# Seven block products in one more output stage, a later query load, and another order in the last stage

## The chip, the core and the metric

The program runs on one core of a Trainium2 chip. Its engines work side by side and wait for each other through semaphores: TensorE (PE, matrix products into the PSUM banks), VectorE (DVE), ScalarE (ACT), GpSimd (POOL) and SyncE (SP). POOL, SP and ACT also issue DMA transfers. The metric is device time in microseconds, the median of several runs of the program. The profile is one execution, whose span runs from its first to its last instruction.

## What is computed

A linear attention with cosine weights feeds a gated feed-forward block. Only what matters here is shown:

```python
def phi(x, c, s):
    r = np.maximum(x, 0.0)
    return np.concatenate([r * c, r * s], axis=-1)
q_p = phi(q, cos_w, sin_w)
k_p = phi(k, cos_w, sin_w)
kv = np.einsum('bhsf,bhsd->bhfd', k_p, v)
z = np.sum(k_p, axis=2)
num = np.einsum('bhsf,bhfd->bhsd', q_p, kv)
den = np.einsum('bhsf,bhf->bhs', q_p, z)[..., None] + 1e-06
attn_out = num / den
x = attn_out.transpose(0, 2, 1, 3).reshape(B * S, H * D)
g = x @ w_gate
silu = g * (1.0 / (1.0 + np.exp(-g)))
val = x @ w_val
out = silu * val @ w_out
```

The batch is 8, the heads 8, the sequence 576, the head dimension 64; so x has 4608 rows of 512, and d_ff is 1536. All inputs and the output are float32; the kernel multiplies in 16 bits.

## The kernel before

The 4608 rows are worked through in nine groups (`tg` 0 to 8) of 512 tokens, each of four tiles of 128. A group has a feed-forward stage of 12 slices (`fc`), which leaves the hidden activations in `ht`, and an output stage, which multiplies `ht` by `w_out` (`wo_sb`). Between the pieces of both, "slots" hang the attention work that the next groups need: 16 slots in a group, 12 in the feed-forward stage and 4 in the output stage. Groups 0 and 1 have a plain output stage, twelve products with 512 columns for each tile:

```python
def ffn_out(t, f0=0, f1=None, queues=None):
    ...
    r = t % OUT * P
    for fc in range(f0, f1):
        nc.tensor.matmul(out=o_ps[t], lhsT=ht[:, fc, r:r + P], rhs=wo_sb[:, fc],
                         start=(fc == 0), stop=(fc == FC - 1))
    ...
    if t % 2 == 0:
        nc.scalar.mul(out=ob_of(t), in_=ps, mul=DOWN)
    else:
        nc.vector.tensor_single_scalar(out=ob_of(t), in_=ps, scalar=DOWN, op=ALU.mult)
    store(t, queues=queues)
```

Groups 2 to 8 split the product into 2 by 2 blocks and form it from seven block products in place of eight (Strassen's method in Winograd's form). This needs four sums of blocks of the weights (`weight_sum`, T1 to T4, once for the kernel) and four sums of blocks of `ht` in each group (`token_sum`, S1 to S4). `HC` is 6, so one `product` is 12 matmuls of 256 columns:

```python
def sums_behind(fc):
    for n, lo, hi in {7: ((3, 0, 4),), 8: ((1, 0, 4),), 9: ((2, 0, 4),), 10: ((4, 0, 4), (3, 4, 6)),
                      11: ((1, 4, 6), (2, 4, 6))}.get(fc, ()):
        token_sum(n, lo, hi)

def out_by_quarters(tg, slot_of):
    last = tg == NTG - 1
    ...
    def product(to, a, b, first):
        for kc in range(HC):
            for i in range(2):
                nc.tensor.matmul(out=to[i][:, 0] if len(to) == 2 else to[0][:, i],
                                 lhsT=a[:, kc, i * P:(i + 1) * P], rhs=b[:, kc], ...)
    ...
    nb = 2 if last else 1
    a = home("a", fills=True)
    product(a, aq[:, 0, 0], bq[:, 0, 0], True)
    b = home("b", nb, seeded=True)
    for p_, o_ in each(b, a[0]):
        nc.scalar.copy(out=p_, in_=o_)
    e = home("e", fills=True)
    product(e, S3, T3, True)
    nc.scalar.mul(out=C22, in_=e[0], mul=DOWN)
    c = home("c", seeded=True)
    free("e")
    product(b, S2, T2, False)
    ...                                     # VectorE: c from C22 and b
    token_sum(4, 0 if tg in GATE else 4, 6)
    slot_of(0)
    product(a, aq[:, 1, 0], bq[:, 1, 0], False)
    copied("act", C11, a)
    free("a")
    if last:
        store_two(t0, slice(0, HD))
    slot_of(1)
    product(b, S1, T1, False)
    ...                                     # VectorE: C22 from b
    if last:
        store_two(t0 + 2, slice(HD, d_model))
    product(c, aq[:, 1, 1], T4, False)
    copied("act", C21, c)
    free("c")
    if last:
        store_two(t0 + 2, slice(0, HD))
    else:
        for t in (t0 + 2, t0 + 3):
            store(t, queues=queues)
    slot_of(2)
    product(b, S4, bq[:, 1, 1], False)
    copied("dve", C12, b)
    ...
    for t in (t0, t0 + 1):
        store(t, *((slice(HD, d_model), (nc.sync, nc.scalar)) if last else (slice(0, d_model), queues)))
    slot_of(3)
```

In the last group `b` lies in two banks, one for each tile of the pair, and `store_two` issues its two transfers on SP and on ACT. The loop over the groups, and the loads that run ahead:

```python
def load_behind(b):
    nc.gpsimd.tensor_copy(out=hold2, in_=phit[b - 1][0:1, :, 0, 0, 0])   # POOL waits for the turned q
    if b < AHEAD:                     # AHEAD = 5
        load(b, "q")
    if b > 3:
        load_kv(b)
    if AHEAD <= b + 1 < B:
        load(b + 1, "q")

for tg in range(1, NTG):
    s0 = SLOTS * tg
    if tg in GATE:                    # 5 to 8: gate product by seven block products too
        if not loose[0]:
            loose[0] = True
            rows[0] = max(used) + 1
        ffn_by_quarters(tg, lambda i: slot(s0 + i))
    for fc in range(FC) if tg not in GATE else ():
        ffn_fc(tg, fc)
        if tg > 1:
            sums_behind(fc)
        slot(s0 + fc)
    if tg > 1:
        out_by_quarters(tg, lambda i: slot(s0 + FC + i))
        continue
    for i in range(OUT):
        ffn_out(tg * OUT + i, queues=(nc.gpsimd, nc.gpsimd))
        weight_sum(i)
        slot(s0 + FC + i)
```

PSUM has eight banks, and `take` deals them out when the program is written. From group 5 on (`loose`) it gives the free bank whose last use, by an estimate kept in rows of work, lies furthest back:

```python
def take(n, hold=None, fills=False, seeded=False):
    taken = {x for r in held.values() for x in r}
    if loose[0]:
        free = [b for b in range(8) if b not in taken]
        if n == 1:
            bs = [min((b for b in free if filled[b] or not seeded), key=lambda b: used[b])]
        else:
            b0 = min((b for b in free if b + 1 in free), key=lambda b: max(used[b:b + 2]))
            bs = [b0, b0 + 1]
    ...
```

Of the kernel before, what the change touches and what calls it, by code (L numbers as in the profile page):

```python
# [18 lines left out]
def kernel(  # L19
# [10 lines left out]
    nc = tc.nc  # L30
    B, H, S, D = q.shape
    P = 128
# [18 lines left out]
    KH = KC // 2  # L51
    GATE = (5, 6, 7, 8)
    AHEAD = 5
    WSUM = (29, 38, 48, 64)
    ROW = {2: ([16, 16, 17, 17], 18, (20, 21, 21, 22), 8), 3: ([12, 12, 13, 13], 18, (17, 20, 21, 21), 6), 4: ([12, 12, 14, 14], 14, (13, 16, 17, 18), 5), 5: ([12, 12, 12, 14], 14, (14, 16, 17, 17), 5), 6: ([6, 8, 11, 12], 12, (13, 14, 15, 18), 3), 7: ([6, 6, 7, 7, 8, 8, 9, 9, 10, 10, 11, 11, 12, 12, 13, 13, 14, 14], 16, (12, 13, 14, 15), 3)}
    TILES = {2: (2, 9, 10, 11), 3: (5, 8, 10, 11), 4: (5, 7, 9, 11), 5: (3, 4, 7, 9), 6: (0, 2, 5, 7), 7: (0, 1, 5, 7), 8: (0, 3, 5, 7)}
    KVONE = (2, 5)
    LATER = {2: (0, 1, 3, 4, 7, 8), 3: (0, 1, 3, 4, 7, 8), 4: (0, 1, 3, 4, 7, 8), 5: (0, 1, 3, 4, 7, 8), 6: (0, 1, 3, 4, 7, 8), 7: (0, 1, 3, 4, 7, 8), 8: (0, 1, 3, 4, 7, 8)}
    LATE = dict(M=44, V=87, O=131, X=26, x=150, v=(190, 250, 120, 150), e=130, a=90, c=170, b=110, k=120)

# [21 lines left out]

    filled = [False] * 8
    loose = [False]
    rows = [0]

    def take(n, hold=None, fills=False, seeded=False):

        taken = {x for r in held.values() for x in r}
        if loose[0]:  # L90
            free = [b for b in range(8) if b not in taken]
            if n == 1:
                bs = [min((b for b in free if filled[b] or not seeded), key=lambda b: used[b])]
            else:
                b0 = min((b for b in free if b + 1 in free), key=lambda b: max(used[b:b + 2]))
                bs = [b0, b0 + 1]
            if hold is not None:
                held[hold] = bs
            for b in bs:
                filled[b] = fills or seeded  # L100
            touch(bs)
            return banks[:, bs[0]] if n == 1 else banks[:, bs[0]:bs[0] + 2]
        free = [b for b in range(0, 8, n) if not any(b <= x < b + n for x in taken)
                and (filled[b] or not seeded)]

        b0 = min(free, key=lambda b: (n == 1 and hold is not None and hold[0] == "o" and b ^ 1 not in taken,
                                      sorted(used[b:b + n], reverse=True)))
        if hold is not None:
            held[hold] = range(b0, b0 + n)
        filled[b0:b0 + n] = [fills or seeded] * n  # L110
        touch(range(b0, b0 + n))
        return banks[:, b0] if n == 1 else banks[:, b0:b0 + n]
# [649 lines left out]
            (queues or (nc.sync, nc.sync))[e].dma_start(out=out_v[idx // NC, idx % NC][:, cols],  # L762
                                                        in_=ob_of(t)[e * SH:(e + 1) * SH, cols])

    def store_two(t, cols):
        for e in range(2):
            (b, c), (b1, _) = divmod(2 * t + e, NC), divmod(2 * t + 2 + e, NC)
            assert b == b1
            (nc.sync, nc.scalar)[e].dma_start(
                out=out_v[b, c:c + 3:2, :, cols].rearrange("c p f -> p c f"),  # L770
                in_=obs[t // 2][e * SH:(e + 1) * SH, :, cols])

# [40 lines left out]
# [8 lines that stand above are left out]
        queues = (nc.gpsimd, nc.gpsimd) if tg > 0 else None  # L821
        t0 = tg * OUT
        for t in (t0, t0 + 2):
            ob_of(t)
        C11, C12 = (obs[t0 // 2][:, :, x * HD:(x + 1) * HD] for x in range(2))
        C21, C22 = (obs[t0 // 2 + 1][:, :, x * HD:(x + 1) * HD] for x in range(2))

        def home(nm, parts=1, **kw):
            return [take(1, ("o", tg, nm, i), **kw).rearrange("p (t x) -> p t x", x=HD) for i in range(parts)]

        def free(nm, parts=1):
            for i in range(parts):
                give_back(("o", tg, nm, i))

        def product(to, a, b, first):
            rows[0] += LATE["O"]
            for kc in range(HC):
                for i in range(2):
                    nc.tensor.matmul(out=to[i][:, 0] if len(to) == 2 else to[0][:, i],  # L839
                                     lhsT=a[:, kc, i * P:(i + 1) * P], rhs=b[:, kc],  # L840
                                     start=first and kc == 0 and i == 0,
                                     stop=kc == HC - 1, skip_group_check=True)

        def each(ps, *others):
            if len(ps) == 1:
                return [(ps[0], *others)]
            return [(ps[i][:, 0:1], *(o[:, i:i + 1] for o in others)) for i in range(2)]

        def copied(eng, o, ps, x=DOWN):
            for p_, o_ in each(ps, o):  # L850
                if eng == "act":
                    nc.scalar.mul(out=o_, in_=p_, mul=x)  # L852
                else:
                    nc.vector.tensor_single_scalar(out=o_, in_=p_, scalar=x, op=ALU.mult)
# [13 lines that stand above are left out]
        for p_, o_, x_ in each(b, c[0], C22):  # L868
            nc.vector.scalar_tensor_tensor(out=o_, in0=x_, scalar=UP, in1=p_, op0=ALU.mult, op1=ALU.add)
# [9 lines that stand above are left out]
        for p_, x_ in each(b, C22):  # L879
            nc.vector.scalar_tensor_tensor(out=x_, in0=p_, scalar=DOWN, in1=x_, op0=ALU.mult, op1=ALU.add)  # L880
        if last:
            store_two(t0 + 2, slice(HD, d_model))
        product(c, aq[:, 1, 1], T4, False)
        copied("act", C21, c)
        free("c")
        if last:
            store_two(t0 + 2, slice(0, HD))
        else:
            for t in (t0 + 2, t0 + 3):
                store(t, queues=queues)  # L890
        slot_of(2)
        product(b, S4, bq[:, 1, 1], False)
        copied("dve", C12, b)
        free("b", nb)
        for t in (t0, t0 + 1):
            store(t, *((slice(HD, d_model), (nc.sync, nc.scalar)) if last else (slice(0, d_model), queues)))
        slot_of(3)
# [31 lines left out]
    def at(s, *fns):  # L929
        plan.setdefault(s, []).extend(fns)  # L930
# [8 lines left out]
    def turn(t, fast=False):  # L939
        return lambda: x_turn(t, fast)  # L940
# [83 lines left out]
    def load_2():  # L1024

        nc.gpsimd.tensor_copy(out=hold2, in_=xT[1][0:1, 0, 0, 0:2])
        for nm in ("k", "v"):
            load(2, nm)

    at((0, 1), turn(4), load_2)  # L1030
    at((1, 0), turn(5), a_(6, 0))
    at((1, 1), a_(6, 1))
# [16 lines left out]
    def load_behind(b):  # L1049

        nc.gpsimd.tensor_copy(out=hold2, in_=phit[b - 1][0:1, :, 0, 0, 0])
        if b < AHEAD:
            load(b, "q")
        if b > 3:
            load_kv(b)
        if AHEAD <= b + 1 < B:
            load(b + 1, "q")

    def load_kv(b):
# [6 lines left out]
        load_kv(3)  # L1066


    for n in range(4):
        at(WSUM[n], lambda n=n: gate_weight_sum(n))  # L1070
    for tg in GATE:
# [31 lines left out]
    for tg in range(1, NTG):  # L1103
        s0 = SLOTS * tg
        if tg in GATE:
# [3 lines that stand above are left out]
            ffn_by_quarters(tg, lambda i: slot(s0 + i))  # L1109
        for fc in range(FC) if tg not in GATE else ():  # L1110
            ffn_fc(tg, fc)
            if tg > 1:
                sums_behind(fc)
            slot(s0 + fc)
        if tg > 1:
            out_by_quarters(tg, lambda i: slot(s0 + FC + i))
            continue
        for i in range(OUT):
            ffn_out(tg * OUT + i, queues=(nc.gpsimd, nc.gpsimd))
            weight_sum(i)  # L1120
            slot(s0 + FC + i)
    assert not plan, sorted(plan)


# [28 lines left out]
```

## Time and profile before

| What | us |
|---|---|
| device time, median of 3 runs (lowest to highest) | 314.07 (313.59 to 314.17) |
| span of the profiled execution | 312.5 |
| TensorE busy | 303.3 |
| VectorE busy | 235.9 |
| ScalarE busy | 154.7 |
| GpSimd busy | 66.0 |

The granted TensorE clock was 0.999 over the span. Busy time is the time in which at least one instruction of an engine was under way. "L839" in a line of the profile is line 839 of the kernel: L605 is the plain feed-forward product, L663 and L676 the gate and value products of groups 5 to 8, L780 the plain output stage, L839 the seven block products of the output stage, L354 the k-by-v product, L485 the q-by-kv product. A wait is put down to the operation that released it.

### The profile page before, as it was taken

Reading aid. Unit: us, or ns where it says so; the run is one execution under the profiler, and the core shown is the slowest. Engines: PE = TensorE matmul, PEld = TensorE weight load, DVE = VectorE, ACT = ScalarE, POOL = GpSimd, SP = SyncE. Lnnn points to the kernel's source line nnn. Section 1 sums busy time; section 2 is a strip of 40 time slices with the busy share of each in tenths; the row PEclk is TensorE's granted clock in tenths of the full one; section 3 lists DMA queues with packets and bytes.
Section 4 is the critical chain, followed back from the end, with each engine's and each line's share of the span. In section 5 each row is a group of like instructions: output and inputs, shape, how many; then the busy total and the mean of one; then the engine's idle time right before and its main releaser. Section 6 shows DMA issues by size and latency. Waiting matters only on the chain.

```text
span 312.5 us, 6945 instructions
## 1 busy us (share of the span) xinstructions
PE 303.3 (97%) x2768; PEld 196.9 (63%) x2768; DVE 235.9 (75%) x474; ACT 154.7 (49%) x294; POOL 66.0 (21%) x118
## 2 busy tenths in 40 slices
PE   8799999999999999999999999999999999999992
PEld 3587465445445486547654686768767876786682
DVE  7774678787876988587887887898789569855771
ACT  7454556673435446435545454778543344334520
POOL 7754202001420405030413031202200220040000
PEclk9999999999999999999999999999999999999999
DMA  7999999998798898979496979790991141022005
GB/s 257 222 198 196 206 205 128 236 134 111 115 235 125 137 186 142 167 107 202 84 187 90 200 124 197 79 149 19 169 135 33 23 131 36 20 63 71 2 1 134
DMA packets 72976, 41.08 MB, mean 131 GB/s; under 512 B 49904, under 2 KB 69872, under 8 KB 72944
## 3 DMA queue, kind: packets, MB, share of 16 engines
q0 software_dynamic: 24880, 24.91, 46.6%
q1 hardware_dynamic: 47472, 15.21, 30.8%
q10 hardware_dynamic: 592, 0.52, 0.6%
q8 instruction: 21, 0.34, 0.4%
q14 instruction: 11, 0.09, 0.1%
HBM read 37.75 MB, written 9.44 MB: 151 GB/s over the span
## 4 chain that ended last, share of the span: by engine, by line
PE 92%; DMA 3%; DVE 2%; SPq 1%; ACT 1%; issue 0%; DVEq 0%; ACTq 0%
PE banks L605 33%; PE banks L839 21%; PE banks L676 13%; PE banks L663 11%; PE banks L780 6%; PE banks L354 3%; DMA ht<-in_k_dram 3%; PE banks L485 2%; PE banks L535 1%; SPq L171 1%; PE banks L466 1%; DVE ht L681 1%; PE banks L577 0%; DVE x L512 0%; ACT phit L417 0%
## 5 line engine op out<-in xcount | busy, mean ns | idle before, releaser
L611 ACT ACTIVATE sg<-banks 128x512 bf16<-128x512 f32 (+2 forms) x68 | 37.2, 548 | 52.4 <-PE banks L605 49.9
L605 PE MATMUL banks<-xT,wg_sb 128*128 128x512 f16 (+2 forms) x272 | 62.0, 354 | 0.0
L605 PE MATMUL banks<-xT,wv_sb 128*128 128x512 f16 (+2 forms) x272 | 62.0, 354 | 0.0
L616 DVE TENSOR_TENSOR ht<-sg,banks 128x512 f16<-128x512 bf16 (+2 forms) x68 | 41.7, 622 | 21.9 <-PE banks L605 15.4
L762 POOL DMA_DIRECT2D out_dram<-ob x56 | 29.5, 534 | 116.8 <-ACT ob L852 111.2
L676 PE MATMUL banks<-xT,wv_sb 128*128 128x512 f16 x192 | 48.6, 379 | 0.0
L605 PEld LDWEIGHTS <-wv_sb 128*128 128x128 f16 x272 | 26.1, 98 | 26.1
L605 PEld LDWEIGHTS <-wg_sb 128*128 128x128 f16 x272 | 24.8, 98 | 21.5
L839 PEld LDWEIGHTS <-ht 128*128 128x128 f16 x336 | 32.8, 98 | 4.8
L681 DVE TENSOR_TENSOR ht<-sg,banks 128x512 f16<-128x512 bf16 x48 | 31.0, 681 | 3.3 <-ACT sg L669 3.3
L676 PEld LDWEIGHTS <-wv_sb 128*128 128x128 f16 x192 | 18.8, 98 | 13.3
L839 PEld LDWEIGHTS <-sums 128*128 128x128 f16 x252 | 24.7, 98 | 2.9
L669 ACT ACTIVATE sg<-banks 128x512 bf16<-128x512 f32 x36 | 20.5, 590 | 11.8 <-PE banks L663 11.8
L780 PE MATMUL banks<-wo_sb,ht 128*128 128x512 f16 x96 | 22.7, 379 | 0.0
L512 DVE TENSOR_TENSOR x<-banks,rec 128x512 f16<-128x512 f32 (+1 forms) x32 | 21.6, 674 | 1.3 <-PE banks L466 0.3
L663 PEld LDWEIGHTS <-wgs_sb 128*128 128x128 f16 x192 | 17.8, 98 | 7.4 <-issue 0.6
L663 PE MATMUL banks<-kvt,wgs_sb 128*128 128x256 f16 x144 | 21.6, 273 | 0.4 <-DVE x L512 0.4
L839 PE MATMUL banks<-wo_sb,ht 128*128 128x256 f16 x168 | 20.6, 273 | 0.0
L304 DVE TENSOR_TENSOR v<-raw_v,tab 128x1152 bf16<-128x1152 bf16 x27 | 19.8, 753 | 0.3 <-ACT raw_v L902 0.3
L839 PE MATMUL banks<-wt_sb,sums 128*128 128x256 f16 x168 | 19.5, 273 | 0.0
L839 PE MATMUL banks<-wt_sb,ht 128*128 128x256 f16 x168 | 19.5, 273 | 0.0
L852 ACT ACTIVATE ob<-banks 128x512 f32<-128x512 f32 x14 | 8.4, 598 | 22.1 <-PE banks L839 19.0
(125 smaller groups left out, 409.0 us busy)
## 6 DMA issues: line engine op xcount, KB each, us to landing
out_dram<-ob POOLq DMA_DIRECT2D x56, 128.0 KB, 4.1
raw_k<-in_k_dram POOLq DMA_DIRECT2D x7, 576.0 KB, 6.0
raw_q<-in_q_dram POOLq DMA_DIRECT2D x6, 576.0 KB, 11.3
raw_v<-in_v_dram POOLq DMA_DIRECT2D x6, 576.0 KB, 9.3
wo_sb<-in_moe_w_out_dram POOLq DMA_DIRECT2D x3, 512.0 KB, 12.8
out_dram<-ob SPq DMA_DIRECT2D x11, 128.0 KB, 5.8
wg_sb<-in_moe_w_gate_dram POOLq DMA_DIRECT2D x5, 256.0 KB, 9.1
wv_sb<-in_moe_w_val_dram POOLq DMA_DIRECT2D x5, 256.0 KB, 9.6
```

Of the source, the lines that this page charges most:

```text
L304: nc.vector.tensor_tensor(out=v2s[b == 1][:, g, :, :, 0:D], in0=(first if b == 0 and g == 0 else {"v": raw_of(b, "v")})["v"][:, g].unsquee ...
L512: nc.vector.tensor_tensor(out=st["x", t].rearrange("p (y e d) -> p e y d", e=2, d=D)[:, :, ys], in0=ps[:, :, 0:2 * J * D1].rearrange("p e ...
L605: nc.tensor.matmul(out=st["f", tg, fc, lo][i], lhsT=(wg_sb, wv_sb)[i][:, kc, fs], rhs=xT[tg][:, ts, kc], start=(kc == 0), stop=(kc == KC - 1))
L611: nc.scalar.activation(out=sg[:, 0:n], in_=st["f", tg, fc, lo][0], func=AF.Silu, scale=DOWN)
L616: nc.vector.tensor_tensor(out=ht[:, fc, r:r + n], in0=st.pop(("s", tg, fc, lo))[:, 0:n], in1=ps[1], op=ALU.mult)
L663: nc.tensor.matmul(out=to[:, i], lhsT=a[:, c, 2 * u + i], rhs=x[:, :, c], start=first and i == 0 and c == 0, stop=c == KH - 1, skip_group_ ...
L669: nc.scalar.activation(out=gates[u, w][:, :, j * HT:(j + 1) * HT], in_=src, func=AF.Silu, scale=DOWN)
L676: nc.tensor.matmul(out=val[u, i, w], lhsT=wv_sb[:, kc, fc * P:(fc + 1) * P], rhs=xT[tg][:, :, kc], start=(kc == 0), stop=(kc == KC - 1))
L681: nc.vector.tensor_tensor(out=ht[:, fc], in0=gates[u, w][:, i], in1=val.pop((u, i, w)), op=ALU.mult)
L762: (queues or (nc.sync, nc.sync))[e].dma_start(out=out_v[idx // NC, idx % NC][:, cols], in_=ob_of(t)[e * SH:(e + 1) * SH, cols])
L780: nc.tensor.matmul(out=o_ps[t], lhsT=ht[:, fc, r:r + P], rhs=wo_sb[:, fc], start=(fc == 0), stop=(fc == FC - 1))
L839: nc.tensor.matmul(out=to[i][:, 0] if len(to) == 2 else to[0][:, i], lhsT=a[:, kc, i * P:(i + 1) * P], rhs=b[:, kc], start=first and kc == ...
```

## The change

Group 1 takes the output stage of seven block products, which spares one block product in eight. Its four weight sums must then be there before the stage begins, so they move from that stage into slots of group 0's output stage and group 1's feed-forward stage (`TSUM`), and group 1's token sums are added behind its slices 7 to 11. The first query load that runs ahead (batch element 5) no longer follows directly on the loads for element 4; it waits until the last turned x tile that group 3 will read, made during group 2, has landed. Four numbered picks of a PSUM bank (`SECOND`) take the second-best bank in place of the best, batch element 4 takes two single banks for its k-by-v product (`KVONE`), and several slots move by one or two. In the last group the block C21 is scaled on VectorE in place of ScalarE, the two stores of C22 are both issued on SP, and the last product is ordered by halves, so that the first of its two banks is complete before the second is begun.

```diff
-    WSUM = (29, 38, 48, 64)
-    ROW = {... 3: ([12, 12, 13, 13], 18, (17, 20, 21, 21), 6), 4: ([12, 12, 14, 14], 14, (13, 16, 17, 18), 5), 5: ([12, 12, 12, 14], 14, (14, 16, 17, 17), 5), ...}
-    TILES = {2: (2, 9, 10, 11), 3: (5, 8, 10, 11), ...}
-    KVONE = (2, 5)
+    WSUM = (31, 38, 48, 64)
+    ROW = {... 3: ([12, 12, 14, 14], 18, (17, 20, 21, 21), 6), 4: ([12, 12, 12, 14], 14, (15, 16, 17, 18), 5), 5: ([12, 12, 12, 14], 15, (14, 16, 16, 17), 4), ...}
+    TILES = {2: (0, 9, 10, 11), 3: (5, 9, 10, 11), ...}
+    SECOND = (31, 37, 38, 79)
+    TSUM = [(2, 2), (2, 3), 18, 19]
+    KVONE = (2, 4, 5)
 ...
+            picks[0] += 1
+            other = picks[0] in SECOND
 ...                                        # n == 1, and the same for a pair
-                bs = [min((b for b in free if filled[b] or not seeded), key=lambda b: used[b])]
+                bs = sorted((b for b in free if filled[b] or not seeded), key=lambda b: used[b])
+                bs = bs[min(other, len(bs) - 1):][:1]
 ...
-        def product(to, a, b, first):
+        def product(to, a, b, first, halves=False):
-            for kc in range(HC):
-                for i in range(2):
+            steps = [(kc, i) for kc in range(HC) for i in range(2)]
+            for kc, i in sorted(steps, key=lambda x: x[1]) if halves else steps:
 ...
-            store_two(t0 + 2, slice(HD, d_model))
+            store_two(t0 + 2, slice(HD, d_model), (nc.sync, nc.sync))
         product(c, aq[:, 1, 1], T4, False)
-        copied("act", C21, c)
+        copied("dve" if last else "act", C21, c)
 ...
-        product(b, S4, bq[:, 1, 1], False)
+        product(b, S4, bq[:, 1, 1], False, last)
 ...
+    for n in range(4):
+        at(TSUM[n], lambda n=n: weight_sum(n))
 ...                                        # in load_behind
-        if AHEAD <= b + 1 < B:
+        if AHEAD < b + 1 < B:
 ...
+    def load_ahead():
+        nc.gpsimd.tensor_copy(out=hold2, in_=xT[AHEAD - 2][0:1, OUT - 1, 0, 0:2])
+        load(AHEAD, "q")
+
+    at(SLOTS * (AHEAD - 3) + FC, load_ahead)
 ...                                        # in the loop over the groups
-            if tg > 1:
-                sums_behind(fc)
+            sums_behind(fc)
             slot(s0 + fc)
-        if tg > 1:
-            out_by_quarters(tg, lambda i: slot(s0 + FC + i))
-            continue
-        for i in range(OUT):
-            ffn_out(tg * OUT + i, queues=(nc.gpsimd, nc.gpsimd))
-            weight_sum(i)
-            slot(s0 + FC + i)
+        out_by_quarters(tg, lambda i: slot(s0 + FC + i))
```

More of the change, by code (lines that the diff above doesn't have):

```diff
@@ L53 @@
     AHEAD = 5
-    WSUM = (29, 38, 48, 64)
-    ROW = {2: ([16, 16, 17, 17], 18, (20, 21, 21, 22), 8), 3: ([12, 12, 13, 13], 18, (17, 20, 21, 21), 6), 4: ([12, 12, 14, 14], 14, (13, 16, 17, 18), 5), 5: ([12, 12, 12, 14], 14, (14, 16, 17, 17), 5), 6: ([6, 8, 11, 12], 12, (13, 14, 15, 18), 3), 7: ([6, 6, 7, 7, 8, 8, 9, 9, 10, 10, 11, 11, 12, 12, 13, 13, 14, 14], 16, (12, 13, 14, 15), 3)}
-    TILES = {2: (2, 9, 10, 11), 3: (5, 8, 10, 11), 4: (5, 7, 9, 11), 5: (3, 4, 7, 9), 6: (0, 2, 5, 7), 7: (0, 1, 5, 7), 8: (0, 3, 5, 7)}
-    KVONE = (2, 5)
+    WSUM = (31, 38, 48, 64)
+    ROW = {2: ([16, 16, 17, 17], 18, (20, 21, 21, 22), 8), 3: ([12, 12, 14, 14], 18, (17, 20, 21, 21), 6), 4: ([12, 12, 12, 14], 14, (15, 16, 17, 18), 5), 5: ([12, 12, 12, 14], 15, (14, 16, 16, 17), 4), 6: ([6, 8, 11, 12], 12, (13, 14, 15, 18), 3), 7: ([6, 6, 7, 7, 8, 8, 9, 9, 10, 10, 11, 11, 12, 12, 13, 13, 14, 14], 16, (12, 13, 14, 15), 3)}
+    TILES = {2: (0, 9, 10, 11), 3: (5, 9, 10, 11), 4: (5, 7, 9, 11), 5: (3, 4, 7, 9), 6: (0, 2, 5, 7), 7: (0, 1, 5, 7), 8: (0, 3, 5, 7)}
+    SECOND = (31, 37, 38, 79)
+    TSUM = [(2, 2), (2, 3), 18, 19]
+    KVONE = (2, 4, 5)
     LATER = {2: (0, 1, 3, 4, 7, 8), 3: (0, 1, 3, 4, 7, 8), 4: (0, 1, 3, 4, 7, 8), 5: (0, 1, 3, 4, 7, 8), 6: (0, 1, 3, 4, 7, 8), 7: (0, 1, 3, 4, 7, 8), 8: (0, 1, 3, 4, 7, 8)}
@@ L84 @@
     loose = [False]
+    picks = [0]
     rows = [0]
@@ L91, in take @@
             free = [b for b in range(8) if b not in taken]
+            picks[0] += 1
+            other = picks[0] in SECOND
             if n == 1:
-                bs = [min((b for b in free if filled[b] or not seeded), key=lambda b: used[b])]
-            else:
-                b0 = min((b for b in free if b + 1 in free), key=lambda b: max(used[b:b + 2]))
+                bs = sorted((b for b in free if filled[b] or not seeded), key=lambda b: used[b])
+                bs = bs[min(other, len(bs) - 1):][:1]
+            else:
+                b0 = sorted((b for b in free if b + 1 in free), key=lambda b: max(used[b:b + 2]))
+                b0 = b0[min(other, len(b0) - 1)]
                 bs = [b0, b0 + 1]
@@ L763, in store, with store_two @@
                                                         in_=ob_of(t)[e * SH:(e + 1) * SH, cols])
-    def store_two(t, cols):
+    def store_two(t, cols, queues=None):
         for e in range(2):
@@ L768, in store_two @@
             assert b == b1
-            (nc.sync, nc.scalar)[e].dma_start(
+            (queues or (nc.sync, nc.scalar))[e].dma_start(
                 out=out_v[b, c:c + 3:2, :, cols].rearrange("c p f -> p c f"),
@@ L833, in free @@
                 give_back(("o", tg, nm, i))
-        def product(to, a, b, first):
+        def product(to, a, b, first, halves=False):
             rows[0] += LATE["O"]
-            for kc in range(HC):
-                for i in range(2):
[L839 to L842, printed above, removed]
+            steps = [(kc, i) for kc in range(HC) for i in range(2)]
+            for kc, i in sorted(steps, key=lambda x: x[1]) if halves else steps:
+                nc.tensor.matmul(out=to[i][:, 0] if len(to) == 2 else to[0][:, i],
+                                 lhsT=a[:, kc, i * P:(i + 1) * P], rhs=b[:, kc],
+                                 start=first and kc == 0 and i == 0,
+                                 stop=kc == HC - 1, skip_group_check=True)
         def each(ps, *others):
```

## The prediction, made before the result was known

> **What bounds the kernel now.** I read the shares of busy time first, then the chain of work in order of time, then TensorE's own waits, and last the timeline of the stages that the change touches.
>
> ```profile
> PE 303.3 (97%) x2768; PEld 196.9 (63%) x2768; DVE 235.9 (75%) x474; ACT 154.7 (49%) x294; POOL 66.0 (21%) x118
> ...
> L780 PE MATMUL banks<-wo_sb,ht 128*128 128x512 f16 x96 | 22.7, 379 | 0.0
> ...
> L839 PE MATMUL banks<-wt_sb,sums 128*128 128x256 f16 x168 | 19.5, 273 | 0.0
> ```
>
> TensorE is the bound: it is busy for 97% of the span, and the chain gives it 92%. The second and third line are the two kinds of output stage. Their means, 379 and 273 ns, are no costs, since neighbours overlap; what a stage costs has to be read as elapsed time, from the chain:
>
> ```profile
> 77.72 10.36 PE banks L780 x48
> ...
> 111.34 9.20 PE banks L839 x84
> ```
>
> The columns are start, length and number of instructions. The first is group 1's plain stage, 48 matmuls in 10.36 us, 216 ns each. The second is group 2's stage of seven block products, 84 in 9.20 us, 109.5 ns each; the later ones read 9.19, 9.17, 9.17, 9.17 and 9.17 us. TensorE's waits are few:
>
> ```profile
> PE banks L441 <- DVE wgs_sb L433: 1.1, 1, 1.1
> PE banks L208 <- DVE zeros L203: 1.0, 1, 1.0
> PE banks L466 <- DVE wt_sb L454: 0.6, 1, 0.6
> PE banks L663 <- DVE x L512: 0.4, 1, 0.4
> PE banks L354 <- DVE ht L681: 0.3, 1, 0.3
> ```
>
> The first three lie in the opening, which the change leaves alone. The last two lie at 191.8 and 193.7 us, in group 5, where TensorE waits for banks that VectorE has not yet read: 0.75 us in all. What is left is the end:
>
> ```profile
> 302.79 2.78 PE L839 MATMUL banks<-wt_sb,ht 128*128 128x256 f16 x24
> 302.99 0.60 ACT L852 ACTIVATE ob<-banks 128x512 f32<-128x512 f32 x1 [2.02 <-PE banks L839]
> 303.61 4.35 SPq L769 DMA_DIRECT2D out_dram<-ob  x3
> 303.62 3.08 ACTq L769 DMA_DIRECT2D out_dram<-ob  x2
> 304.19 0.76 DVE L880 SCALAR_TENSOR_TENSOR ob<-banks,ob 128x256 f32<-128x256 f32 x2 [0.72 <-PE banks L839]
> ...
> 305.41 1.47 PE L839 MATMUL banks<-wo_sb,sums 128*128 128x256 f16 x12
> 306.74 0.60 ACT L852 ACTIVATE ob<-banks 128x512 f32<-128x512 f32 x1 [3.15 <-issue]
> 306.81 0.76 DVE L854 TENSOR_SCALAR ob<-banks 128x256 f32<-128x256 f32 x2 [1.87 <-PE banks L839]
> 307.37 0.64 ACTq L769 DMA_DIRECT2D out_dram<-ob  x1
> 308.06 1.20 SPq L762 DMA_DIRECT2D out_dram<-ob  x2
> 308.10 1.45 ACTq L762 DMA_DIRECT2D out_dram<-ob  x2
> ```
>
> TensorE ends at 306.88, the span at 312.5: a tail of 5.6 us. The product for C21 is done at about 305.5, yet ScalarE scales it at 306.74, because its queue was busy with stores from 303.62 to 306.70. So C21's stores are issued at 307.37, the four stores of C12 queue behind them, and the last begins at 309.00 (the ACT pair is 0.80 and 0.55 us). VectorE had C12 ready at 307.57.
>
> [...] Here one issue is 0.55 to 0.66 us on either queue (one took 2.36), and four in a row are much of the tail.
>
> **Part 1, group 1's output stage.** It trades 48 matmuls of 10.36 us for 84 of 9.19 us: **−1.17 us**, straight on the path, if TensorE isn't held. Its sums are on VectorE, so I walked VectorE's queue through the end of group 1, whose times before are (slices 7 and 8, the casts of the k-by-v product, slices 9 and 11):
>
> ```profile
> 70.04 1.28 DVE L616 TENSOR_TENSOR ht<-sg,banks 128x512 f16<-128x512 bf16 x2
> 71.74 1.23 DVE L380 CAST kv<-banks 64x130 bf16<-64x130 f32 x4 [0.42 <-PE banks L354]
> 73.60 0.69 DVE L616 TENSOR_TENSOR ht<-sg,banks 128x512 f16<-128x512 bf16 x1 [0.64 <-PE banks L605]
> ...
> 77.57 0.69 DVE L616 TENSOR_TENSOR ht<-sg,banks 128x512 f16<-128x512 bf16 x1 [0.26 <-PE banks L605]
> ```
>
> Start to start, a slice's product takes 0.61 us, a sum of 1024 elements 0.61, one of 512 about 0.38 (so in group 2), and an x tile 1.04. Slice 7 then ends at 70.65, its sum at 71.26, slice 8 at 71.87, the next sum at 72.48, the casts at 73.7, slice 9 at 74.3, its sum at 74.9, an x tile at 75.95, slice 10 at 76.55, two sums at 77.55, an x tile at 78.6, slice 11 at 79.2, the last two sums at about 79.95. The first product needs only even slices, the second S3, which is there at 77.55. The third needs S2, at 77.72 + 2 × 1.31 = 80.34. So VectorE is 0.4 us early, and in group 2, at the same point, it is as early (113.4 for 113.96). The weight sums, 4 × 0.95 us, fall where VectorE has room: an idle 1.24 us before 54.54, then slices 0 to 4 with idle stretches of 0.6 to 1.1 us. I add nothing for them.
>
> **Part 2, the last stage.** With C21 on VectorE, which is free from 304.95, it is ready at 305.5 + 0.69 = 306.2, its stores go out at about 306.25 instead of 307.37 and end at 306.9. Both stores of C22 lie on SP, at 304.97 and 305.6, done by 306.2, so that ACT isn't held by them. The first half of the last product is complete at 305.41 + 6 × 0.109 = 306.06, its copy of 0.42 us ends at 306.6; the second copy, at TensorE's end, ends at 307.25. The C12 stores then start at 306.95 and 307.55 on each queue, and the last at 307.6 instead of 309.00: 1.4 us. The transfers get denser: about 1 MB must leave after 305, and the DMA engines moved at most 276 GB/s in any microsecond there, so I keep **−1.2 us**. TensorE's work in this stage stays 84 matmuls.
>
> **Part 3, the held load, the slots and the bank picks.** The load for element 5 was issued at 104.72, right behind three loads of 576 KB, and is used by ScalarE only in group 3's output stage, at 143 us. Held until group 3's last x tile has landed, at about 117, it has some 25 us for 7 to 11 us of transfer. It relieves the transposes of x in group 2, but no TensorE wait stands there: 0. Of the 0.75 us of waits in group 5, none of the four altered picks falls on the bank concerned (counting calls, that is about the 12th to 14th in group 5; the altered are 31, 37, 38 and 79). But the order of use with which group 5 starts is new, as are its slots in group 4. I give it four chances in ten, so **−0.3 us**.
>
> The sum is −1.17 − 1.2 − 0.3 = −2.67, and 314.07 − 2.67 = 311.40. The time outside the span, 1.6 us, stays.
>
> **Rivals.** (A) VectorE becomes the bound at the end of group 1: my margin is only 0.4 us on a walk with some ten steps. If a matmul waits for S2 or for a bank, 0.3 to 1 us is lost of part 1, and the time is 311.7 to 312.4. The 75% busy VectorE and 86% in the stretch from 71.7 to 79.2 speak for it, group 2, which is as full and has no wait, against. (B) The tail is set by transfers, not issues: if landing rather than issue sets the end, denser stores land 0.5 to 1 us later than I assume, and the time is 311.9 to 312.4. For it speaks that the DMA engines are at 0.97 from 309 to 310; against, that they are at 0.37 in the microsecond before. (C) The new bank order makes new waits in groups 5 to 8, or the shifted schedule lets a q or x transpose land late; four hand-chosen picks show how sensitive this is. Each wait seen is 0.3 to 0.4 us; three would make it 312.5. (D) The group 5 waits vanish whole, as the slots were retuned as a set: 310.95.
>
> **Range and chances.** The two large parts are mechanical, and the rivals cost more than (D) adds. I take 311.4, with 310.4 to 312.9 eight times in ten. Two per cent, 6.3 us, is more than all parts together, and a loss of that size would need a wait in every group: faster 0.01, within 2% 0.985, slower 0.005.
>
> **What would show it.** Right: a chain without L780 in group 1 but an L839 piece of 84 near 9.2 us there, no wait of TensorE for `sums`, `wt_sb` or `ob`; C21's scaling on VectorE before 306.3 on the old clock of time, less part 1; the last store issued within 0.8 us of TensorE's end (2.1 before); a tail of 4.2 to 4.5 us instead of 5.6. Wrong: a group 1 stage over 9.6 us, more or longer waits of TensorE than two beyond the opening, or a tail over 5 us although the issues are early.

## The result and the profile after

The changed kernel takes 311.62 us (311.47 to 311.79) against 314.06 us before: a ratio of 0.9924, 95% interval 0.9912 to 0.9937. The forecast was 311.4. The span of the profiled execution fell from 312.5 to 309.8 us.

The lines of the changed kernel that answer to those shown of before are these: from the page the busy shares, from the chain in order of time group 1's and group 2's output stages (start, length, number of matmuls; L846 is now the seven block products), and TensorE's waits (total, times, longest).

```profile
PE 302.2 (98%) x2804; PEld 200.5 (65%) x2804; DVE 240.9 (78%) x486; ACT 155.5 (50%) x297; POOL 67.7 (22%) x119
```

```profile
77.58 9.17 PE banks L846 x84
...
110.01 9.19 PE banks L846 x84
```

```profile
PE banks L215 <- DVE zeros L210: 1.0, 1, 1.0
PE banks L448 <- DVE wgs_sb L440: 0.7, 1, 0.7
PE banks L473 <- DVE wt_sb L461: 0.6, 1, 0.6
PE banks L670 <- DVE x L519: 0.4, 1, 0.4
```

Group 1's stage starts almost where it did (77.58 for 77.72) and takes 9.17 us in place of 10.36. Of the two waits in group 5 the one of 0.33 us is gone, the one of 0.42 us is still there. The timeline of the last stage:

```profile
301.84 3.31 SPq L776 DMA_DIRECT2D out_dram<-ob  x4
301.84 3.36 ACTq L776 DMA_DIRECT2D out_dram<-ob  x2
302.42 0.76 DVE L887 SCALAR_TENSOR_TENSOR ob<-banks,ob 128x256 f32<-128x256 f32 x2 [0.73 <-PE banks L846]
303.63 1.47 PE L846 MATMUL banks<-wo_sb,sums 128*128 128x256 f16 x12
303.83 1.08 DVE L861 TENSOR_SCALAR ob<-banks 128x512 f32<-128x512 f32 x2 [0.66 <-PE banks L846]
305.14 0.42 DVE L861 TENSOR_SCALAR ob<-banks 128x256 f32<-128x256 f32 x1 [0.23 <-PE banks L846]
305.24 1.21 SPq L769 DMA_DIRECT2D out_dram<-ob  x2
305.29 1.43 ACTq L769 DMA_DIRECT2D out_dram<-ob  x2
```

TensorE ends at 305.10, and the span 4.70 us later; before it was 5.62. (The span is read to 0.1 us, so such a tail is good to about 0.05.) The stores of C12 go out 0.14 us after TensorE's end (1.18 before).

So the 2.7 us of span come out as follows: group 1's stage 1.19 (10.36 − 9.17); the tail 0.92 (5.62 − 4.70); group 5's wait 0.33; about 0.3 in the opening, where the change does nothing and where the wait for the first casts of q is 1.06 us before, 0.70 here and 1.0 in the kernel with twelve operations more; less 0.2 that was newly lost in group 1's slices. Some 0.15 us is left over, within the rounding. That loss is here, in TensorE's and VectorE's timelines of the changed kernel:

```profile
72.98 0.64 PE L492 MATMUL banks<-kv,phit 128*128 128x65 bf16 x8
```

```profile
71.48 0.69 DVE L818 TENSOR_TENSOR ht<-ht 128x1024 f16<-128x1024 f16 x1
72.08 1.23 DVE L387 CAST kv<-banks 64x130 bf16<-64x130 f32 x4
```

The same eight matmuls take 0.42 us elsewhere. They need the casts, which end at 73.31, because a new token sum at 71.48 stands ahead of them; before, the casts ended at 72.97.

### The profile page after: what moved, and what is told of

It reads as the page before. It is cut to its first block, busy times and chain, and to the rows that moved or that the text cites. A ratio compares the mean times of both kernels' runs of the same rounds, so it can differ in the third digit from the quotient of the medians.

```text
span 309.8 us, 7026 instructions
## 1 busy us (share of the span) xinstructions
PE 302.2 (98%) x2804; PEld 200.5 (65%) x2804; DVE 240.9 (78%) x486; ACT 155.5 (50%) x297; POOL 67.7 (22%) x119
## 4 chain that ended last, share of the span: by engine, by line
PE 92%; DVE 5%; ACT 2%; issue 1%; DVEq 0%; ACTq 0%
PE banks L612 31%; PE banks L846 24%; PE banks L683 13%; PE banks L670 12%; PE banks L787 3%; PE banks L492 2%; PE banks L361 2%; DVE v L311 1%; PE banks L542 1%; PE banks L473 1%; PE banks L215 1%; DVE ht L623 1%; PE banks L416 0%; PE banks L584 0%; ACT L247 0%
## 5 line engine op out<-in xcount | busy, mean ns | idle before, releaser
L846 PEld LDWEIGHTS <-ht 128*128 128x128 f16 x384 | 37.4, 98 | 5.4
L846 PEld LDWEIGHTS <-sums 128*128 128x128 f16 x288 | 28.2, 98 | 3.3
L846 PE MATMUL banks<-wo_sb,ht 128*128 128x256 f16 x192 | 23.6, 273 | 0.0
L846 PE MATMUL banks<-wt_sb,ht 128*128 128x256 f16 x192 | 22.3, 273 | 0.0
L846 PE MATMUL banks<-wt_sb,sums 128*128 128x256 f16 x192 | 22.3, 273 | 0.0
L301 DVE TENSOR_TENSOR r_q<-raw_q,tab 128x1152 bf16<-128x1152 bf16 x20 | 14.4, 754 | 5.1 <-ACT raw_q L284 4.7
```

The lines of the kernel that those rows point to most:

```text
L301: nc.vector.tensor_tensor(out=st[b, "q"][:, g], in0=o.unsqueeze(2).to_broadcast([P, NC, 2, D]), in1=tab, op=ALU.mult)
```

## The experiments

Each kernel was timed beside the kernel before, and its ratio is to that. Two questions were open: which of the many edits keep TensorE from waiting, and what shortened the tail. "The tail" is the time from TensorE's end to the span's end in the profile.

**The last stage alone.** The kernel before with the three edits of the last stage:

```diff
-            store_two(t0 + 2, slice(HD, d_model))
+            store_two(t0 + 2, slice(HD, d_model), (nc.sync, nc.sync))
-        copied("act", C21, c)
+        copied("dve" if last else "act", C21, c)
-        product(b, S4, bq[:, 1, 1], False)
+        product(b, S4, bq[:, 1, 1], False, last)
```

> The kernel before with the three edits of the last stage alone. My theory: the last stage gives about 0.9 us by itself, as the tail from TensorE's end to the span's end shrinks from 5.6 to about 4.7 us: 313.1. Rival (the gain is in group 1, and the tail is set by the landing of the transfers, which only looks shorter in one profile): under 0.3 us, 313.8 or more.

313.24 us, ratio 0.9979 (0.9973 to 0.9985); the tail is 4.72 us. As expected, but the first store on ACT still takes 2.20 us, as long as before, only nothing waits behind it.

**The seven block products alone.** The kernel before with group 1's stage, its sums and the moved weight sums (`TSUM`), nothing else:

```diff
+    TSUM = [(2, 2), (2, 3), 18, 19]
+    for n in range(4):
+        at(TSUM[n], lambda n=n: weight_sum(n))
-            if tg > 1:
-                sums_behind(fc)
+            sums_behind(fc)
-        if tg > 1: ... out_by_quarters, otherwise ffn_out and weight_sum
+        out_by_quarters(tg, lambda i: slot(s0 + FC + i))
```

> The kernel before with the seven block products in group 1, its sums and the moved weight sums, and nothing else: old slots, old bank picks, load for element 5 not held, old last stage. My theory: group 1's output stage takes 9.2 us in place of 10.4, about 0.2 us is lost in group 1's slices where TensorE waits for the casts of the k-by-v product, and the rest of the schedule only shifts: about 1.0 us, 313.1. Rival (the slots, bank picks and the held load are needed to keep the gain): new waits of TensorE in groups 3 to 8 eat half of it or more, 313.6 to 314.5.

314.26 us, ratio 1.0004 (0.9996 to 1.0012): nothing is gained, and the rival was right that the slots are needed. But the large wait is in group 1's own stage and not in the groups that the rival named. VectorE's and TensorE's timelines in group 1's stage show why:

```profile
82.62 1.42 DVE L295 TENSOR_TENSOR r_q<-raw_q,tab 128x1152 bf16<-128x1152 bf16 x2
83.95 0.95 DVE L639 TENSOR_TENSOR wgs_sb<-wg_sb 128x1536 f16<-128x1536 f16 x1
84.82 1.42 DVE L295 TENSOR_TENSOR r_q<-raw_q,tab 128x1152 bf16<-128x1152 bf16 x2
86.16 0.69 DVE L881 SCALAR_TENSOR_TENSOR ob<-banks,ob 128x512 f32<-128x512 f32 x1
```

```profile
86.90 1.47 PE L840 MATMUL banks<-wo_sb,sums 128*128 128x256 f16 x12 [1.41 <-DVE ob L881]
```

The update of C22 (L881) must read bank `b` before the last product may add to it. It stands behind a gate weight sum and two q products that hang on slots of the same stage, and TensorE waits 1.41 us, more than the stage saves. A second new wait, 0.43 us at 256.3 in group 7, is looked at below. Unexpectedly, the tail is 4.62 us, although the last stage is the old one. It hides a loss: TensorE ends at 307.79, 0.91 us later than before.

**The same with two slots moved.** Of the moved slots only these:

```diff
-    WSUM = (29, 38, 48, 64)
+    WSUM = (31, 38, 48, 64)
-    ROW = {... 3: ([12, 12, 13, 13], 18, ...
+    ROW = {... 3: ([12, 12, 14, 14], 18, ...
```

> The kernel before with the seven block products in group 1 and two of the moved slots: the gate weight sum of slot 29 goes to 31, and the second pair of q products for element 3 from slot 13 to 14. My theory: the whole 1.41 us wait for the C22 update in group 1's output stage came from these two standing ahead of that update in VectorE's queue; the stage takes 9.2 us, the later wait of 0.4 us in group 7 stays, and the time is 0.9 to 1.2 us under the kernel with the block products alone: 313.1 to 313.3. Rival (VectorE is simply too full in that stage): the wait moves to the next operation, 313.8 or more.

313.14 us, ratio 0.9978 (0.9969 to 0.9987). From the chain of this kernel:

```profile
77.54 9.17 PE banks L840 x84
```

The wait is gone whole. It was the order in VectorE's queue, and not VectorE's load. The two slots are worth about 1.1 us (314.26 to 313.14), as much as the block products themselves. The wait in group 7 stays, and there is a new one of 0.3 us for a turned x tile. The tail is again short, and against the kernel before TensorE ends only 0.31 us earlier (306.57 for 306.88); the rest of this kernel's gain over it is the tail, which is explained below.

**The best bank at every pick.** The changed kernel with

```diff
-    SECOND = (31, 37, 38, 79)
+    SECOND = ()
```

> The changed kernel, but every bank pick takes the bank that the estimate calls best. My theory: the picks spare one or two waits of 0.3 to 0.4 us each in groups 5 to 7, where the estimate errs: 312.0 to 312.4. Rival (they do nothing measurable): 311.6, within 0.2.

312.13 us, ratio 0.9946 (0.9927 to 0.9965). TensorE has one more wait in the profile than in the changed kernel:

```profile
254.68 0.42 PE L492 MATMUL banks<-kv,phit 128*128 128x65 bf16 x8 [0.43 <-DVE ht L688]
```

It is the wait of group 7 that also came with the block products alone and that the kernel before did not have. The altered picks step round it. That the other order of takes in group 1 shifts which bank is oldest six groups later is likely, but no run shows it. The wait of 0.33 us in group 5 is gone in this kernel too, and in the next one, so neither the picks nor the held load removed it; one of the other moved slots or the two single banks did, and these weren't separated. The profile accounts for 0.43 us; the medians differ by 0.5, while the intervals of the two ratios overlap.

**The load not held.** The changed kernel with the query load for element 5 behind those for element 4, as before:

```diff
-        if AHEAD < b + 1 < B:
+        if AHEAD <= b + 1 < B:
-    at(SLOTS * (AHEAD - 3) + FC, load_ahead)
```

> The changed kernel, but the query load for element 5 goes out right behind those for element 4, as before. My theory: no TensorE wait depends on it, 311.6, within 0.2 us. Rival (it keeps 576 KB out of the way of the transposes of x in group 2): TensorE waits at the start of group 3 for a turned x tile, 0.3 to 2 us, 311.9 to 313.6.

312.00 us, ratio 0.9939 (0.9920 to 0.9957), single runs from 311.51 to 314.76. The profiled execution has no wait of TensorE in groups 1 to 8 that the changed kernel lacks. Whether the hold narrows the spread or gains anything isn't settled.

**The parts of the last stage, one by one, in the changed kernel.** C21 on ScalarE again:

```diff
-        copied("dve" if last else "act", C21, c)
+        copied("act", C21, c)
```

> The changed kernel, but C21 of the last group is scaled on ScalarE again; the stores of C22 stay on SP. My theory: what held ScalarE was the store of C22 in its queue, which is gone from it, so C21 is scaled as early as on VectorE and the time is 311.7, within 0.2. Rival (the engine is what counts): ScalarE's first store of the kernel, recorded at 2.36 us in the kernel before, still holds its queue, C21 comes 0.5 us late or more, and the tail grows from 4.7 to 5.2 us or more: 312.1 to 312.4.

311.53 us, ratio 0.9917 (0.9903 to 0.9932), tail 4.61. The last product in the old order:

```diff
-        product(b, S4, bq[:, 1, 1], False, last)
+        product(b, S4, bq[:, 1, 1], False)
```

> The changed kernel with the last product in the old order, both banks complete only at its end. My theory: the two copies of 0.42 us (start to start 0.34) then both follow TensorE's end, so C12's first stores start some 0.3 us later and the last 0.3: 311.9. Rival (the queues of SP and ACT, busy with C21 until 0.1 us after TensorE's end, set the start anyway): 311.6, within 0.15.

311.81 us, ratio 0.9926 (0.9909 to 0.9942), tail 4.65. C12's first stores begin 0.38 us after TensorE's end in place of 0.14, and the tail is not longer; the last store begins at the same point, 1.09 us after it for 1.07. The stores of C22 on two queues:

```diff
-            store_two(t0 + 2, slice(HD, d_model), (nc.sync, nc.sync))
+            store_two(t0 + 2, slice(HD, d_model))
```

> The changed kernel with the two stores of C22 on SP and ACT, as before; C21 stays on VectorE. My theory: with the scaling off ScalarE it does no harm that ACT waits in a store: 311.6, within 0.2. Rival (ACT's store of C22 holds its store of C21 and then those of C12): 0.3 us or more, 311.9 to 312.4.

311.52 us, ratio 0.9928 (0.9910 to 0.9946), tail 4.63. None of the three parts can be told from nothing.

**All three parts undone.**

> The changed kernel with the last stage as it was before: C21 on ScalarE, C22's stores on SP and ACT, the last product not by halves. Theory now: the long tail of the kernel before came from one store on ACT that took 2.36 us, at the moment at which an instruction fetch of 10 KB runs, and in every kernel without that the tail is 4.6 to 4.7 us whatever the order in the stage, as the transfers set it; so 311.6, within 0.2, tail 4.6 to 4.8. Rival (my prediction: the order of the stage is worth about 1 us): 312.5 or more, tail 5.5.

311.58 us, ratio 0.9922 (0.9909 to 0.9936), tail 4.64. With the whole last stage as it was, the time is that of the changed kernel. Its timeline:

```profile
301.80 2.01 ACTq L776 DMA_DIRECT2D out_dram<-ob  x2
303.59 1.47 PE L846 MATMUL banks<-wo_sb,sums 128*128 128x256 f16 x12
303.85 0.60 ACT L859 ACTIVATE ob<-banks 128x512 f32<-128x512 f32 x1 [2.08 <-PE banks L846]
...
305.44 1.14 SPq L769 DMA_DIRECT2D out_dram<-ob  x2
305.45 1.40 ACTq L769 DMA_DIRECT2D out_dram<-ob  x2
```

ScalarE scales C21 at 303.85, 0.26 us after the last product began; in the kernel before it was 1.33 us after. ACT's two stores take 2.01 us here and 3.08 before, because the first of them lasts 0.74 us and not 2.36. So what differs is that one store. In the kernel before, the DMA view of the tenth of a microsecond from 303.90, 0.37 us after that store began, has this on a queue that the view names for instructions (such a packet is called a fetch below):

```profile
q14 instruction: 1, 0.01, 34.3%
```

**Three, then twelve operations more.** The kernel before with operations of one element, whose results nobody reads, that are meant only to shift the place of later instructions:

```diff
+    def three_more():
+        for _ in range(3):
+            nc.scalar.activation(out=tiny, in_=half_pi, func=AF.Silu)
+
+    at(40, three_more)
```

> The kernel before with three more ScalarE operations of one element each, about 0.2 us, in group 2, where ScalarE is a third busy; nothing else. Theory now: they move the place at which ScalarE's instruction fetch falls, the first store of the last stage takes 0.74 us instead of 2.36, and the tail shrinks from 5.6 to 4.6 us: 313.1 to 313.4, faster with more work. Rival (the long store belongs to that stage's order, or to something other than ScalarE's place in its instructions): 314.1 or a little more.

313.98 us, ratio 1.0003 (0.9995 to 1.0011), as the rival said. The store takes 2.21 us, the tail is 5.53, and the fetch has not moved: it falls into the tenth from 303.80, again 0.37 us after the store began. But the edit did not shift ScalarE's instructions. With the three operations, three separate semaphore waits at L611 went; the kernel before and this one have there:

```profile
L611 ACTq EVENT_SEMAPHORE  x54: 17/17/1913, 20.8 to 175.2; - x54
```

```profile
L611 ACTq EVENT_SEMAPHORE  x51: 17/17/1914, 20.7 to 175.1; - x51
```

Both traces hold 6945 instructions, and counted in the trace, with waits and DMA issues, the first store of the last stage is ScalarE's 448th instruction in both. So this run doesn't speak against the theory. Next, both engines that compute in this stage were given more:

```diff
+    tiny2 = consts.tile([P, 1], FP32)
+
+    def two_more():
+        nc.scalar.activation(out=tiny, in_=half_pi, func=AF.Silu)
+        nc.vector.memset(tiny2, 0.0)
+
+    for s in range(96, 108):
+        at(s, two_more)
```

> The kernel before with twelve more operations of one element on ScalarE (0.2 us each) and twelve on VectorE (0.06 us each), one of each in twelve slots of group 6; nothing else. Theory: the place of an engine's instruction fetch moves by twelve instructions, away from the first store of the last stage, which then takes 0.74 us; the tail falls from 5.6 to about 4.7 us and the time to 313.0 to 313.4 although work was added. Rival (the long store has another cause, or the three operations tried earlier show that the fetch goes with the store): the store stays over 2 us, 314.0 to 314.5.

313.44 us, ratio 0.9981 (0.9974 to 0.9989): faster with 24 operations more. ScalarE now has nine recorded instructions more (three waits went again), and its first store is the 457th. The last fetch on that queue now falls into the microsecond from 297, before the stage's stores, and the old last stage reads:

```profile
303.48 2.00 ACTq L769 DMA_DIRECT2D out_dram<-ob  x2
305.28 1.47 PE L839 MATMUL banks<-wo_sb,sums 128*128 128x256 f16 x12
305.53 0.60 ACT L852 ACTIVATE ob<-banks 128x512 f32<-128x512 f32 x1 [2.08 <-PE banks L839]
```

The first store takes 0.74 us, the tail 4.65. The gain, about 0.5 us by the medians, is less than the 0.97 us by which the tail shrank in the profile; TensorE also has a new wait of 0.2 us for a turned x.

**A sum later, and fewer stores.** The changed kernel with S1 behind slice 9, and with one store for each tile of C12:

```diff
-        for n, lo, hi in {7: ((3, 0, 4),), 8: ((1, 0, 4),), 9: ((2, 0, 4),), ...
+        for n, lo, hi in {7: ((3, 0, 4),), 8: ((1, 0, 4),) if early else (),
+                          9: ((2, 0, 4),) if early else ((1, 0, 4), (2, 0, 4)), ...
...
+    def store_one(t, cols, queue):
+        (b, c), (b1, c1) = divmod(2 * t, NC), divmod(2 * t + 1, NC)
+        queue.dma_start(out=out_v[b, c:c + 2, :, cols], in_=ob_of(t)[:, cols])
```

> The changed kernel with two additions: in group 1 the sum S1 is formed behind slice 9 in place of slice 8, so that the casts of the k-by-v product come first in VectorE's queue; and each tile of C12 goes out by one store of both halves in place of two, one on SP and one on ACT. Theory: the 0.2 us that TensorE loses in group 1 before its first q-by-kv product is gone; the tail stays at 4.6 to 4.7 us, as transfers set it and not issues: 311.4. Rival (issues set the end): the last issue begins some 0.5 us earlier and the tail falls to 4.2 or less, 310.9.

316.92 us, ratio 1.0105 (1.0089 to 1.0120), tail 9.84: neither theory nor rival. The casts now come in time, and the eight matmuls at 73.07 take 0.42 us again, but the delay comes back in the output stage, where the second product waits:

```profile
79.02 2.78 PE L852 MATMUL banks<-wt_sb,sums 128*128 128x256 f16 x24 [0.25 <-DVE x L519]
```

The wait was only moved: of the 5.70 us of the chain from 73.27 to 78.97 us VectorE has 4.97. The tail comes from the stores. Of some microseconds after TensorE's end, the last three columns are the granted clock, the DMA share and GB/s:

```profile
308.00:309.00 1.00, 0.00 (x0) 0.00 (x0) 0.00 (x0) 0.00 (x0) 0.00 (x0) 0.74 0.10 17
309.00:310.00 1.00, 0.00 (x0) 0.00 (x0) 0.00 (x0) 0.00 (x0) 0.00 (x0) 0.50 0.14 45
310.00:311.00 1.00, 0.00 (x0) 0.00 (x0) 0.00 (x0) 0.00 (x0) 0.00 (x0) 0.50 0.13 43
```

A share of 0.14 is about two of the 16 engines (0.14 × 16 = 2.2). The outermost dimension of the store's target is 2, the two halves. In the changed kernel, which sends each half by a store of its own, the share stays between 0.76 and 1.05 for the 2.5 us after TensorE's end. In the last stage the two kernels differ in C12's stores alone, in their number and shape, so the low share goes with one of these; how isn't shown. So this kernel doesn't tell whether fewer issues would shorten the tail. No kernel tried beats the changed one clearly.

## Why the prediction was right, and where only by luck

**The number** was right: 311.62 for 311.40, inside the range. Its three parts fared differently.

**Part 1** (−1.17 us) was right in size: the stage fell by 1.19 us, and the last sums were ready in time for the third product. Two things were missing. The walk itself had the casts ending 0.7 us later than before and did not ask who waits for them; the q-by-kv product did, by 0.2 us. And it stopped at the third product. Behind it lay the place where the stage did stall, the update of C22; "I add nothing" for the moved slots was wrong as a statement about them, since two of them carry all of the gain (314.26 without, 313.14 with them). The changed kernel had both moves, so the sum did not suffer; that is luck. Rival A named the right engine, but the wrong operation and the wrong cause: its queue's order, not its load (VectorE is busy for 6.04 of the 7.5 us from 71.7 to 79.2, 81% and not the 86% that the prediction gives).

**Part 2** (−1.2 us) came near in size by luck. The tail shrank by 0.92 us, to 4.70 and not to the 4.2 to 4.5 forecast, and the step that failed is that "its queue was busy with stores": the queue was not busy with an ordinary load of stores, it was held by one store of 2.36 us, which the prediction saw, put in brackets, and did not ask about. Without that store the old order of the stage has the short tail as well. The tails, ACT's first store, and the place of this store among ScalarE's recorded instructions, side by side:

| Kernel | tail, us | ACT's first store, us | its place |
|---|---|---|---|
| before | 5.62 | 2.36 | 448 |
| before, three ScalarE operations more | 5.53 | 2.21 | 448 |
| before, new last stage | 4.72 | 2.20 | 448 |
| before, twelve operations more on each of two engines | 4.65 | 0.74 | 457 |
| block products alone, old last stage | 4.62 | 0.74 | 452 |
| changed, old last stage | 4.64 | 0.74 | 446 |
| changed | 4.70 | 0.74 | 446 |

Either takes the microsecond away: the new last stage, because nothing urgent waits behind the long store, or a change that moves the fetch (0.74 us in the last four rows). In the changed kernel both are there, so the edits of the last stage gain nothing there: group 1's other instructions had moved the fetch already. That the fetch makes the store long rests on three things. It begins 0.37 us into the store in the first three rows, and in the others it doesn't fall into that store. It goes with ScalarE's program: in all fourteen kernels the last fetch begins when ScalarE has begun 446 to 450 of its recorded instructions (VectorE 629 to 650 of its own), and the first store is long in exactly the three kernels in which it is the 448th. And the twelve added operations moved the fetch and shortened the store without touching the stage. Nearness alone did no harm: in the changed kernel with C21 on ScalarE the last fetch begins 0.04 us after the next store on ACT (304.54), and that store takes 0.66 us. Why the first store takes 2 us when the fetch itself takes 0.35 to 0.55 us isn't shown.

The other step of part 2, that the last issue sets the end, had its size wrong. The last store began 1.07 us after TensorE's end in place of the 0.7 forecast: ACT's first store of C12 took 0.78 us where the walk allowed 0.6, although the prediction had read 0.80 for the same store before (its "0.55 to 0.66 us on either queue" leaves that one out). The step itself is not refuted. In thirteen kernels the span ends 3.5 to 3.6 us after the last store began: with that start 1.02 to 1.09 us after TensorE's end the tail is 4.6 to 4.7 us (eleven kernels), with 1.96 and 2.11 us it is 5.5 and 5.6 (three operations more, and before). The exception is the kernel with fewer stores. For rival B speaks that in the changed kernel, the one without halves and the one with two slots moved, the half microseconds from 2.0 us before TensorE's end to 2.5 after it show a DMA share of 0.5 to 1.05 without a gap. As the last store begins at the same point in all three, they can't tell issue from transfer; that stays open.

**Part 3** (−0.3 us) was right in size: 0.33 of the 0.75 us in group 5 went. It was wrong to give the bank picks nothing: without them there is a new wait of 0.43 us in group 7, which is the kind of wait that rival C described. For the held load 0 stands, unsettled.

## What to carry to other kernels

When a stage is replaced by one with inner dependencies, walk the helper engine's queue through the stage's own hand-overs and not only up to its start; what hangs on the slots inside it may cost as much as the replacement gains. If one instruction in the trace takes several times as long as its likes, find out why before forecasting from it: a cure may be only a shift of something that the next edit shifts as well. Undo each part of a bundle in the changed kernel as well as trying it alone, for two parts may remove the same wait. And look in the trace whether an edit meant to shift instructions has shifted them; three added operations had not.

## What the runs showed of the hardware that was not expected

The first store issued on ACT takes 0.73 to 0.75 us in eleven kernels and 2.20 to 2.36 us in the three where a fetch on an instruction queue begins 0.37 us after its start. Adding 24 operations without use made a kernel faster, with a ratio of 0.9981 (0.9974 to 0.9989), while three added operations left ScalarE with as many instructions as before, as three separate waits went. Fetches on this queue, q14, come all through the kernel before, 11 from 24.2 to 304.0 us, of 8 KB each (0.09 MB in all; the 10 KB of an expectation is the 0.01 MB that the view gives for one). And two stores over 128 partitions whose target has an outermost dimension of 2 together moved 43 to 48 GB/s, where in the changed kernel the stores of half a tile together moved up to 346 GB/s in half a microsecond.
